# Attention over batches beside an MLP stream on one core: earlier DMA transposes, stores on another queue, single q buffers, a rebalanced start

## The chip, the core and the metric

The kernel runs on one core of a Trainium2 chip. The metric is device microseconds of one execution (us). Most executions of a kernel agree closely; this kernel before the change spreads from 360.9 to 368.7 us. On one core a run counts as slow when it lies over 1.5% above the fastest of the same kernel.

## The reference

Linear attention with cosine and sine weights for 8 batches and 8 heads, sequence 576, head dimension 64, then a low-rank token mixer and a two-layer MLP with a residual. All inputs and outputs are float32.

```python
theta = np.pi / 2.0 * np.arange(S) / S
phi = lambda x: concat([relu(x) * cos(theta), relu(x) * sin(theta)], -1)   # 64 -> 128
q_p, k_p = phi(q), phi(k)                      # (8, 8, 576, 128)
kv  = einsum('bhsf,bhsd->bhfd', k_p, v);  z = sum(k_p, axis=2)
x   = (q_p @ kv) / (q_p . z + 1e-6)            # -> (8, 576, 512)
u   = x + ((x.T @ U) @ V).T                    # rank 32 over the sequence
out = u + relu(u @ w_ch1) @ w_ch2              # 512 -> 2048 -> 512
```

## The kernel before

A main stream of 288 slots runs the MLP on TensorE. Each pair of batches has 72 slots: 32 of `g1_main` (u times w1), 4 of `g1_tail`, 36 of `g2_part` (times w2). After each slot the program may put pieces of a later batch's attention: this is what a plan like `(w + o, thunk)` says, where `w` is the slot at which the batch's `kv` product is placed and `o` the offset. The engines only wait for each other where data or buffers ask for it.

For one batch the chain is: loads of k, v, q; VectorE and ScalarE make `k_p` and `q_p`; `q_p` is transposed by DMA into `q_pT`; TensorE makes `kv`, then `x` from `q_pT` and `kv`, then `A` and `u`; `u_bf` is transposed by DMA into `uT`, which the main stream reads. Both DMA transposes are issued by SyncE.

```python
def alloc_q(b):
    qst[b] = pool.tile([P, H, 4, D], FP32, tag="qst", bufs=2, name="qst")
    qt[b] = pool.tile([P, H, D], FP32, tag="qt", bufs=2, name="qt")
# ... q_p has bufs=1, q_pT bufs=1, kst bufs=2, vst bufs=1
def qtr_dma(b, c0, c1):                      # utr_dma: the same for u_bf -> uT
    # ... c0 < 4:
        nc.sync.dma_start_transpose(
            out=q_pT[b][:, c0:c1, :, :].rearrange("f c h t -> f (c h) t"),
            in_=q_p[b][:, c0:c1, :, :].rearrange("p c h f -> p (c h f)"))
# ... at the end of g2_part: o_sb = u + o_ps, then
            nc.sync.dma_start(out=out[b, 0:512, :]..., in_=o_sb)

def loads(b, eng):                           # kk, vv, qq: a tail and a main load each
    # ... qq(): alloc_q(b); load_tail(qt[b], q, b, eng); load_main(qst[b], q, b, eng=eng)
    return kk, vv, qq

def attention_plan(b):
    plan = [(-6, lambda: v_prep(b))]         # casts of v on GpSimd
    for n, c in enumerate(ORD):
        plan.append((-6 + n, lambda c=c: k_prep(b, c, (V_, V_))))
        plan.append((-6 + n, lambda c=c: q_prep(b, c, (A_, None))))
        plan.append((-5 + n, lambda c=c: q_prep(b, c, (None, A_))))
    plan.append((-3, lambda: qtr_dma(b, 4, 5)))
    plan.append((-1, lambda: qtr_dma(b, 0, 2)))
    plan.append((1, lambda: qtr_dma(b, 2, 4)))
    # ... kv_unit at 0 and 2, x_unit from 6, A_unit at 16, u_unit from 18, utr_dma at 20, 24, 28
    if b + 1 < B:
        for at, t in zip((-5, -2, 2), loads(b + 1, G_)):   # on GpSimd's queue
            plan.append((at, t))
    return plan
# ...
for b, w in ((2, 34), (3, 50), (4, 106), (5, 122), (6, 178), (7, 194)):
    for o, t in attention_plan(b):
        put(w + o, t)
```

Of the kernel before, what the change touches and what calls it, by code (L numbers as in the profile page):

```python
# [10 lines left out]
FP32 = mybir.dt.float32  # L11
# [6 lines left out]
def kernel(  # L18
# [14 lines left out]
    H = 8  # L33
# [34 lines left out]
        vt[b] = pool.tile([P, H, D], FP32, tag="vt", bufs=1, name="vt")  # L68

    def alloc_q(b):  # L70
        qst[b] = pool.tile([P, H, 4, D], FP32, tag="qst", bufs=2, name="qst")
        qt[b] = pool.tile([P, H, D], FP32, tag="qt", bufs=2, name="qt")

    def load_main(dst, src, b, h0=0, h1=H, eng=None):
        (eng or nc.sync).dma_start(
# [88 lines left out]
    V_.memset(q_tl, 0.0)  # L164
    V_.memset(q_tlT, 0.0)
    V_.memset(x_tl, 0.0)
    V_.memset(U_bf, 0.0)
    V_.memset(V_bf, 0.0)

# [67 lines left out]

    def qT_alloc(b):
        if b not in q_pT:
            q_pT[b] = pool.tile([P, 4, H, P], BF16, tag="q_pT", bufs=1, name="q_pT")  # L240

    def qtr_unit(b, c, h0=0, h1=H, eng=None, tag="T", bufs=1):
        qT_alloc(b)
# [39 lines left out]
    def den_unit(b, h0, h1, tag, bufs):  # L283
        n = h1 - h0
        d_ps = ps.tile([P, 5, n], FP32, tag=tag, bufs=bufs, name="d_ps")
        for c in range(5):
            for h in range(h0, h1):
                nc.tensor.matmul(
                    out=d_ps[:, c, h - h0 : h - h0 + 1],
                    lhsT=qT_of(b, c, h),  # L290
                    rhs=kv_sb[b][:, h, D:E],
                    start=True,
                    stop=True,
                )
        rec = pool.tile([P, 5, n], FP32, tag="rec5", bufs=2, name="rec5")
        recip(rec[:, 0:4, :], d_ps[:, 0:4, :])
        recip(rec[tail(b), 4, :], d_ps[tail(b), 4, :])
        return rec

    def xh_unit(b, c, h0, h1, rec, tag, bufs):  # L300
# [183 lines left out]
    def g2_part(pr, cc, part):  # L484

        if part == 0:
            o_ps[pr, cc] = ps.tile([P, DM], FP32, tag="o", bufs=2, name="o_ps")
        o = o_ps[pr, cc]
        if cc == 4:
            lhs, c = hid_tl[pr], 0  # L490
        else:
            b, c = (2 * pr, cc) if cc < 4 else (2 * pr + 1, cc - 5)
            lhs = hid[b]
        for j in range(part * 4, part * 4 + 4):
            nc.tensor.matmul(  # L495
                out=o,
                lhsT=lhs[:, j, c * P : c * P + P],
                rhs=w2_bf[:, j, :],
                start=(j == 0),
                stop=(j == NJ - 1),  # L500
            )
        if part < 3:
            return
        o_sb = pool.tile([P, DM], FP32, tag="o_sb", bufs=3, name="o_sb")
        u = u_tl[pr] if cc == 4 else u_bf[b][:, c, :]
        nc.vector.tensor_tensor(out=o_sb, in0=u, in1=o, op=ALU.add)  # L506
        if cc == 4:
            for i in range(2):
                nc.sync.dma_start(
                    out=out[2 * pr + i, 512:S, :], in_=o_sb[i * TS : i * TS + TS, :]  # L510
                )
        else:
            nc.sync.dma_start(
                out=out[b, 0:512, :].rearrange("(p c) n -> p c n", c=4)[:, c, :], in_=o_sb
            )

# [20 lines left out]

    def attention_plan(b):

        plan = [(-6, lambda: v_prep(b))]  # L540
        for n, c in enumerate(ORD):
            plan.append((-6 + n, lambda c=c: k_prep(b, c, (V_, V_))))
            plan.append((-6 + n, lambda c=c: q_prep(b, c, (A_, None))))
            plan.append((-5 + n, lambda c=c: q_prep(b, c, (None, A_))))
        plan.append((-3, lambda: qtr_dma(b, 4, 5)))
        plan.append((-1, lambda: qtr_dma(b, 0, 2)))
        plan.append((1, lambda: qtr_dma(b, 2, 4)))
        plan.append((0, lambda: kv_unit(b, 0, "T", 1)))
        plan.append((2, lambda: kv_unit(b, 1, "T", 1)))
        for n, c in enumerate(ORD):  # L550
            plan.append((6 + 2 * n, lambda c=c: x_unit(b, c, "X", 1)))
        plan.append((16, lambda: A_unit(b, "T", 1)))
        for n, c in enumerate(ORD):
            plan.append((18 + 2 * n, lambda c=c: u_unit(b, c, "T", 1)))
        if b % 2 == 1:
            plan.append((20, lambda: utr_dma(b, 4, 5)))
        plan.append((24, lambda: utr_dma(b, 0, 2)))
        plan.append((28, lambda: utr_dma(b, 2, 4)))
        if b + 1 < B:
            for at, t in zip((-5, -2, 2), loads(b + 1, G_)):  # L560
                plan.append((at, t))
        return plan


    l1 = loads(1, nc.sync)
    for c in ORD:
        k_prep(0, c, (V_, A_), 0, 4)
    l1[0]()
    for c in ORD:
        q_prep(0, c, (V_, A_), 0, 4)  # L570
    v_prep(0, 0, 4, ORD)
    cast_uv()
    for c in ORD:
        qtr_unit(0, c, 0, 4, A_, "g", 3)
    for c in ORD:
        k_prep(0, c, (V_, A_), 4, 8)
    kv_unit(0, 0, "T", 1)
    for c in ORD:
        q_prep(0, c, (V_, A_), 4, 8)
    l1[2]()  # L580
    rec0 = den_unit(0, 0, 4, "X", 1)
    v_prep(0, 4, 8, ORD, (G_, A_, G_, A_, G_))
    w1_load(0)
    w1_load(1)
    l1[1]()
    for c in ORD[:3]:
        qtr_unit(0, c, 4, 8, A_, "g", 3)
    for c in ORD[:2]:
        xh_unit(0, c, 0, 4, rec0, "o", 2)
    for c in ORD[3:]:  # L590
        qtr_unit(0, c, 4, 8, A_, "g", 3)
    for c in ORD[2:]:
        xh_unit(0, c, 0, 4, rec0, "o", 2)
    kv_unit(0, 1, "T", 1)
    rec1 = den_unit(0, 4, 8, "X", 1)
    a0 = A_unit(0, "X", 1, A_, 0, 256)
    for c in ORD[:4]:
        xh_unit(0, c, 4, 8, rec1, "o", 2)
    for d in range(2):
        uTd_open(0, d, "g", 3)  # L600
        uTd_close(0, d, A_)
    xh_unit(0, 3, 4, 8, rec1, "o", 2)
    uTd_open(0, 2, "g", 3)
    uTd_open(0, 3, "o", 2)
    A_unit(0, "X", 1, V_, 256, 512, a0)
    uTd_close(0, 2, V_)
    uTd_close(0, 3, A_)
    w1_load(2)
    v_prep(1, 0, 8, ORD)
    w1_load(3)  # L610
    for n in range(4):
        w2_load(n)
# [5 lines left out]
        beside.setdefault(j, []).extend(thunks)  # L618

    for n, c in enumerate(ORD):  # L620
        at((0, 0, 1, 1, 2)[n], lambda c=c: k_prep(1, c, (V_, A_)))
        at((3, 4, 5, 6, 7)[n], lambda c=c: q_prep(1, c, (V_, A_)))
        ev = V_ if n % 2 else A_
        tg = ("T", 1) if n % 2 else ("o", 2)
        at((4, 5, 6, 7, 8)[n], lambda c=c, ev=ev, tg=tg: qtr_unit(1, c, eng=ev, tag=tg[0], bufs=tg[1]))
    at(9, lambda: kv_unit(1, 0, "o", 2), lambda: kv_unit(1, 1, "o", 2))
# [2 lines left out]
    xt = (("X", 1), ("o", 2), ("T", 1), ("o", 2), ("X", 1))  # L629
    for n, c in enumerate(ORD):  # L630
        at(10 + n // 2, lambda c=c, t=xt[n]: xh_unit(1, c, 0, 8, rec["r"], *t))
    at(12, lambda: uTd_open(1, 0, "o", 2), lambda: uTd_open(1, 1, "o", 2))
    at(13, lambda: A_unit(1, "T", 1))
    at(13, lambda: uTd_close(1, 0, V_), lambda: uTd_close(1, 1, V_))
    at(14, lambda: uTd_open(1, 2, "o", 2), lambda: uTd_open(1, 3, "X", 1))
    at(14, lambda: uTd_close(1, 2, V_), lambda: uTd_close(1, 3, V_))

    slots, todo = [], {}
    for pr in range(NPAIR):
# [15 lines left out]
        put(18 + n, lambda b=b, c=c: u_unit(b, c, "T", 1))  # L655
    for n, t in enumerate(loads(2, G_)):
        put(16 + n, t)
    for b, w in ((2, 34), (3, 50), (4, 106), (5, 122), (6, 178), (7, 194)):
        for o, t in attention_plan(b):
            put(w + o, t)  # L660
    for i, s in enumerate(slots):
# [33 lines left out]
```

## Time and profile before

| | before |
|---|---|
| median of all its runs at the first comparison (lowest to highest) | 365.44 us (360.90 to 368.74) |
| profiled run: time, span, mean granted TensorE clock (1 is full speed) | 362.37 us, 360.6 us, 0.980 |
| TensorE busy | 316.4 us, 88% of the span |
| `x_ps` on TensorE waiting for `q_pT` | 9.8 us, longest 5.2 |
| `q_pT` transposes, issue to landing (min / median / max) | 4.3 / 5.7 / 15.0 us |
| `uT` transposes, the same | 3.0 / 3.1 / 5.5 us |
| loads by GpSimd, median us to landing: k, v, q | 7.7, 10.4, 12.6 |

How to read it: TensorE is the bound almost throughout, so what counts is where it stands still and where it runs at a lower clock. The main stream makes a natural ruler. I take the time of the first matmul of a slot, and compare slot by slot between kernels.

### The profile page before, as it was taken

The page shows a single profiled execution, that of the slowest core. Times are in us where ns is not written, and L with a number is a line of the kernel's source. Part 1 is how long each engine was busy: PE and PEld are TensorE (multiplying, and loading weights), DVE is VectorE, ACT ScalarE, POOL GpSimd, SP SyncE. Part 2 cuts the span into 40 slices and gives each one's busy share as a digit, 9 for nine tenths or more (in the row PEclk, how much of TensorE's full clock was granted, in tenths as well). Part 3 has the DMA queues.
Part 4 walks back from the last instruction along what each step waited for, and adds up shares of the span by engine and source line. Part 5 has one row for each costly group of instructions (what it writes and reads, how often), then busy time and mean ns, then how long its engine had stood idle before and what let it go on. Part 6 is the DMA issues. An engine that isn't in the chain of part 4 may idle for free.

```text
span 360.6 us, 5601 instructions
## 1 busy us (share of the span) xinstructions
PE 316.4 (88%) x2281; PEld 164.8 (46%) x2281; DVE 148.1 (41%) x328; ACT 146.5 (41%) x256; POOL 66.8 (19%) x109
## 2 busy tenths in 40 slices
PE   0678688999768899999989699999989999999995
PEld 0564354446334444446534344446534444464442
DVE  5645236571753755200585546100585750001121
ACT  3935752569050004769350004669700026661000
POOL 5610920629224300200422300000000000000000
PEclk9999899999969999999999989999999999999999
DMA  8999599599979973634949944004546431000221
GB/s 221 274 264 221 84 198 292 148 299 188 321 197 235 298 167 90 178 99 46 257 106 271 271 131 94 9 0 49 134 93 140 114 97 36 0 0 31 87 84 64
DMA packets 65929, 53.08 MB, mean 147 GB/s; under 512 B 45712, under 2 KB 55984, under 8 KB 65904
## 3 DMA queue, kind: packets, MB, share of 16 engines
q1 hardware_dynamic: 55648, 26.75, 32.1%
q0 software_dynamic: 10256, 25.98, 28.0%
q8 instruction: 18, 0.29, 0.4%
q14 instruction: 7, 0.06, 0.0%
HBM read 36.86 MB, written 9.44 MB: 128 GB/s over the span
## 4 chain that ended last, share of the span: by engine, by line
PE 65%; DMA 14%; ACT 9%; DVE 8%; issue 2%; POOL 0%; SPq 0%; ACTq 0%; DVEq 0%; POOLq 0%
PE g_ps L452 27%; PE o_ps L495 25%; DMA q_pT<-q_p 12%; ACT q_p L195 4%; DMA qt<-in_q_dram 2%; PE a_ps L350 2%; PE va_ps L367 2%; DVE k_p L197 2%; PE kv_ps L229 2%; PE gt_ps L470 2%; PE x_ps L324 2%; ACT hid L459 1%; PE t_ps L246 1%; ACT k_p L195 1%; DVE x_bf L310 1%
## 5 line engine op out<-in xcount | busy, mean ns | idle before, releaser
L459 ACT ACTIVATE hid<-g_ps 128x512 bf16<-128x512 f32 x128 | 76.2, 595 | 140.5 <-PE g_ps L452 140.5
L495 PE MATMUL o_ps<-w_bf,hid 128*128 128x512 bf16 x512 | 122.8, 387 | 0.0
L452 PE MATMUL g_ps<-uT,w_bf 128*128 128x512 bf16 x512 | 117.7, 382 | 0.2
L452 PEld LDWEIGHTS <-w_bf 128*128 128x128 bf16 x512 | 49.9, 98 | 59.9 <-issue 3.5
L495 PEld LDWEIGHTS <-hid 128*128 128x128 bf16 x512 | 48.4, 100 | 53.1 <-issue 3.9
L506 DVE TENSOR_TENSOR o_sb<-u_bf,o_ps 128x512 f32<-128x512 bf16 x32 | 21.9, 684 | 58.1 <-PE o_ps L495 58.1
L105 DVE CAST kv<-kv_ps 128x260 bf16<-128x260 f32 x16 | 6.8, 428 | 64.0 <-PE kv_ps L229 64.0
L368 DVE TENSOR_TENSOR u_bf<-x_bf,va_ps 128x512 bf16<-128x512 bf16 x32 | 22.0, 687 | 22.9 <-PE va_ps L367 22.9
L105 POOL CAST v_ext<-vst 128x512 bf16<-128x512 f32 (+1 forms) x34 | 19.9, 626 | 53.6 <-DMA vst<-in_v_dram 39.3
L195 ACT ACTIVATE q_p<-qst,cosw 128x512 bf16<-128x512 f32 x24 | 17.1, 714 | 20.9 <-DMA q_pT<-q_p 20.9
L195 ACT ACTIVATE q_p<-qst,sinw 128x512 bf16<-128x512 f32 (+1 forms) x36 | 23.4, 666 | 0.0
L324 PE MATMUL x_ps<-kv,q_pT 128*128 128x65 bf16 x192 | 10.8, 200 | 10.6 <-DMA q_pT<-q_p 9.8
L470 PE MATMUL gt_ps<-uT_tl,w_bf 128*128 128x128 bf16 x256 | 16.4, 219 | 2.1 <-ACT hid L459 2.0
L324 PEld LDWEIGHTS <-q_pT 128*128 128x128 bf16 x192 | 9.3, 103 | 18.5 <-DMA q_pT<-q_p 11.3
L229 PE MATMUL kv_ps<-v_ext,k_p 128*128 128x65 bf16 x256 | 12.9, 199 | 4.9 <-DVE A_sb L105 2.4
L470 PEld LDWEIGHTS <-w_bf 128*128 128x128 bf16 x256 | 15.1, 98 | 4.0 <-issue 2.3
L334 DVE TENSOR_TENSOR x_bf<-x_ps,rec 128x512 bf16<-128x512 f32 x24 | 16.6, 691 | 0.8
L197 DVE TENSOR_SCALAR k_p<-kst,cosw 128x512 bf16<-128x512 f32 (+1 forms) x36 | 15.9, 462 | 1.7 <-DMA kst<-in_k_dram 1.5
L229 PEld LDWEIGHTS <-k_p 128*128 128x128 bf16 x256 | 11.8, 102 | 8.3 <-DVE A_sb L105 3.9
L495 PE MATMUL o_ps<-w_bf,hid_tl 128*128 128x512 bf16 x64 | 15.4, 379 | 0.0
L367 PE MATMUL va_ps<-A_sb,V_bf 128*128 128x512 bf16 x40 | 15.1, 378 | 0.0
L246 PE MATMUL t_ps<-ident,q_tl 128*128 128x128 bf16 x16 | 2.0, 276 | 13.7 <-ACT q_tl L195 13.7
(92 smaller groups left out, 251.4 us busy)
## 6 DMA issues: line engine op xcount, KB each, us to landing
out_dram<-o_sb SPq DMA_DIRECT2D x32, 256.0 KB, 2.3
kst<-in_k_dram POOLq DMA_DIRECT2D x6, 1024.0 KB, 7.7
vst<-in_v_dram POOLq DMA_DIRECT2D x6, 1024.0 KB, 10.4
qst<-in_q_dram POOLq DMA_DIRECT2D x6, 1024.0 KB, 12.6
w_bf<-in_moe_w_ch_dram POOLq DMA_DIRECT2D x8, 512.0 KB, 11.0
kst<-in_k_dram SPq DMA_DIRECT2D x2, 512.0 KB, 7.4
qst<-in_q_dram SPq DMA_DIRECT2D x2, 512.0 KB, 8.5
vst<-in_v_dram SPq DMA_DIRECT2D x2, 512.0 KB, 11.0
```

The costliest lines, as they stand in the source:

```text
L105: eng.tensor_copy(out=o, in_=i)
L195: nc.scalar.activation(out=o, in_=i, func=AF.Relu, bias=0.0, scale=w)
L197: eng.tensor_scalar(out=o, in0=i, scalar1=0.0, scalar2=w, op0=ALU.max, op1=ALU.mult)
L229: nc.tensor.matmul(out=acc[:, i, :], lhsT=k_p[b][:, c, h, :] if c < 4 else k_tl[:, h, :], rhs=vx[:, c, h, :], start=(c == 0), stop=(c == 4),)
L324: nc.tensor.matmul(out=acc[:, g, i * E : i * E + E], lhsT=qT_of(b, c, h), rhs=kv_sb[b][:, h, :], start=True, stop=True,)
L367: nc.tensor.matmul(out=va, lhsT=V_bf[:, c, :], rhs=A_sb[b], start=True, stop=True)
L368: nc.vector.tensor_tensor(out=u_bf[b][:, c, :] if c < 4 else u_tl[b // 2][rows, :], in0=x_of(b, c, rows), in1=va[rows, :], op=ALU.add,)
L452: nc.tensor.matmul(out=g_ps.rearrange("p (c t) -> p c t", c=4), lhsT=w1_bf[:, d, j * P : j * P + P], rhs=uT[b][:, :, d, :], start=(d == 0) ...
L459: nc.scalar.activation(out=hid[b][:, j, :], in_=g_ps, func=AF.Relu, bias=0.0, scale=1.0)
L470: nc.tensor.matmul(out=g_ps[:, jj, :], lhsT=w1_bf[:, d, j * P : j * P + P], rhs=uT_tl[pr][:, d, :], start=(d == 0), stop=(d == 3),)
L495: nc.tensor.matmul(out=o, lhsT=lhs[:, j, c * P : c * P + P], rhs=w2_bf[:, j, :], start=(j == 0), stop=(j == NJ - 1),)
L506: nc.vector.tensor_tensor(out=o_sb, in0=u, in1=o, op=ALU.add)
```

## The change

Its intent: get the q transposes issued 16 to 24 slots before their first use instead of 9 to 11; keep SyncE's queue for them by moving the stores to ScalarE's queue; pay for a second `q_pT` buffer by giving up the second buffers of `qst` and `qt`; shorten the start by moving work between engines and keep TensorE's clock up with matmuls on zeros.

```diff
     def alloc_q(b):
-        qst[b] = pool.tile([P, H, 4, D], FP32, tag="qst", bufs=2, name="qst")
-        qt[b] = pool.tile([P, H, D], FP32, tag="qt", bufs=2, name="qt")
+        qst[b] = pool.tile([P, H, 4, D], FP32, tag="qst", bufs=1, name="qst")
+        qt[b] = pool.tile([P, H, D], FP32, tag="qt", bufs=1, name="qt")
@@ qT_alloc
-            q_pT[b] = pool.tile([P, 4, H, P], BF16, tag="q_pT", bufs=1, name="q_pT")
+            q_pT[b] = pool.tile([P, 4, H, P], BF16, tag="q_pT", bufs=2, name="q_pT")
@@ g2_part (both stores)
-            nc.sync.dma_start(
+            nc.scalar.dma_start(
@@ attention_plan
-        plan = [(-6, lambda: v_prep(b))]
+        p0 = {2: -14, 3: -14}.get(b, -20 if b % 2 == 0 else -16)
+        plan = [(p0, lambda: v_prep(b))]
         # ... k_prep and q_prep at p0 + n instead of -6 + n (batch 2: half of q_prep on VectorE)
-        plan.append((-3, lambda: qtr_dma(b, 4, 5)))
-        plan.append((-1, lambda: qtr_dma(b, 0, 2)))
-        plan.append((1, lambda: qtr_dma(b, 2, 4)))
+        plan.append((p0 + 2, lambda: qtr_dma(b, 4, 5)))
+        plan.append((p0 + 4, lambda: qtr_dma(b, 0, 2)))
+        plan.append((p0 + 6, lambda: qtr_dma(b, 2, 4)))
         # ... x from 4 (was 6), A at 14 (16), u at 16 + n (18 + 2n), utr at 18, 20, 22 (20, 24, 28)
-            for at, t in zip((-5, -2, 2), loads(b + 1, G_)):
+            for at, t in zip((-13, -12, -8) if b == 2 else (-4, 0, 4), loads(b + 1, G_)):
@@ placing
-    for b, w in ((2, 34), (3, 50), (4, 106), (5, 122), (6, 178), (7, 194)):
+    for b, w in ((2, 38), (3, 54), (4, 88), (5, 124), (6, 160), (7, 196)):
@@ start (cut: about 60 lines)
+    def keep_warm(n, tag, bufs):             # n matmuls of 512 columns on zeros
+    keep_warm(10, "X", 1)
         # ... 2, 3 and 3 more; v casts and evictions of batch 0 moved between ScalarE, VectorE
         # and GpSimd; k_prep(1) before slot 0; one reciprocal per den_unit instead of two
```

More of the change, by code (lines that the diff above doesn't have):

```diff
@@ L166 @@
     V_.memset(x_tl, 0.0)
+    zero = const.tile([P, 512], BF16)
+    G_.memset(zero, 0.0)
+    def keep_warm(n, tag, bufs):
+        w_ps = ps.tile([P, 512], FP32, tag=tag, bufs=bufs, name="w_ps")
+        for _ in range(n):
+            nc.tensor.matmul(out=w_ps, lhsT=zero[:, 0:P], rhs=zero, start=True, stop=True)
     V_.memset(U_bf, 0.0)
@@ L295, in den_unit @@
         rec = pool.tile([P, 5, n], FP32, tag="rec5", bufs=2, name="rec5")
-        recip(rec[:, 0:4, :], d_ps[:, 0:4, :])
-        recip(rec[tail(b), 4, :], d_ps[tail(b), 4, :])
+        recip(rec, d_ps)
         return rec
@@ L512, in g2_part @@
         else:
-            nc.sync.dma_start(
+            nc.scalar.dma_start(
                 out=out[b, 0:512, :].rearrange("(p c) n -> p c n", c=4)[:, c, :], in_=o_sb
@@ L538, in attention_plan @@
     def attention_plan(b):
-        plan = [(-6, lambda: v_prep(b))]
+        p0 = {2: -14, 3: -14}.get(b, -20 if b % 2 == 0 else -16)
+        plan = [(p0, lambda: v_prep(b))]
         for n, c in enumerate(ORD):
-            plan.append((-6 + n, lambda c=c: k_prep(b, c, (V_, V_))))
-            plan.append((-6 + n, lambda c=c: q_prep(b, c, (A_, None))))
-            plan.append((-5 + n, lambda c=c: q_prep(b, c, (None, A_))))
-        plan.append((-3, lambda: qtr_dma(b, 4, 5)))
-        plan.append((-1, lambda: qtr_dma(b, 0, 2)))
-        plan.append((1, lambda: qtr_dma(b, 2, 4)))
+            plan.append((p0 + n, lambda c=c: k_prep(b, c, (V_, V_))))
+            if b == 2:
+                plan.append((p0 + n, lambda c=c: q_prep(b, c, (V_, A_))))
+            else:
+                plan.append((p0 + n, lambda c=c: q_prep(b, c, (A_, None))))
+                plan.append((p0 + n + 1, lambda c=c: q_prep(b, c, (None, A_))))
+        plan.append((p0 + 2, lambda: qtr_dma(b, 4, 5)))
+        plan.append((p0 + 4, lambda: qtr_dma(b, 0, 2)))
+        plan.append((p0 + 6, lambda: qtr_dma(b, 2, 4)))
         plan.append((0, lambda: kv_unit(b, 0, "T", 1)))
@@ L550, in attention_plan @@
         for n, c in enumerate(ORD):
-            plan.append((6 + 2 * n, lambda c=c: x_unit(b, c, "X", 1)))
-        plan.append((16, lambda: A_unit(b, "T", 1)))
+            plan.append((4 + 2 * n, lambda c=c: x_unit(b, c, "X", 1)))
+        plan.append((14, lambda: A_unit(b, "T", 1)))
         for n, c in enumerate(ORD):
-            plan.append((18 + 2 * n, lambda c=c: u_unit(b, c, "T", 1)))
+            plan.append((16 + n, lambda c=c: u_unit(b, c, "T", 1)))
         if b % 2 == 1:
-            plan.append((20, lambda: utr_dma(b, 4, 5)))
-        plan.append((24, lambda: utr_dma(b, 0, 2)))
-        plan.append((28, lambda: utr_dma(b, 2, 4)))
+            plan.append((18, lambda: utr_dma(b, 4, 5)))
+        plan.append((20, lambda: utr_dma(b, 0, 2)))
+        plan.append((22, lambda: utr_dma(b, 2, 4)))
         if b + 1 < B:
-            for at, t in zip((-5, -2, 2), loads(b + 1, G_)):
+            for at, t in zip((-13, -12, -8) if b == 2 else (-4, 0, 4), loads(b + 1, G_)):
                 plan.append((at, t))
@@ L571 @@
     v_prep(0, 0, 4, ORD)
-    cast_uv()
+    w1_load(0)
     for c in ORD:
@@ L576 @@
         k_prep(0, c, (V_, A_), 4, 8)
+    keep_warm(2, "o", 2)
     kv_unit(0, 0, "T", 1)
@@ L580 @@
     l1[2]()
+    keep_warm(3, "o", 2)
     rec0 = den_unit(0, 0, 4, "X", 1)
-    v_prep(0, 4, 8, ORD, (G_, A_, G_, A_, G_))
-    w1_load(0)
+    v_prep(0, 4, 8, ORD, (G_, G_, V_, G_, V_))
+    cast_uv()
     w1_load(1)
     l1[1]()
-    for c in ORD[:3]:
-        qtr_unit(0, c, 4, 8, A_, "g", 3)
+    keep_warm(3, "o", 2)
     for c in ORD[:2]:
         xh_unit(0, c, 0, 4, rec0, "o", 2)
-    for c in ORD[3:]:
-        qtr_unit(0, c, 4, 8, A_, "g", 3)
+    for n, c in enumerate(ORD):
+        qtr_unit(0, c, 4, 8, (A_, A_, V_, A_, V_)[n], "g", 3)
     for c in ORD[2:]:
@@ L594 @@
     kv_unit(0, 1, "T", 1)
+    k_prep(1, 4, (V_, A_))
+    uTd_open(0, 0, "g", 3)
+    uTd_open(0, 1, "g", 3)
     rec1 = den_unit(0, 4, 8, "X", 1)
-    a0 = A_unit(0, "X", 1, A_, 0, 256)
-    for c in ORD[:4]:
-        xh_unit(0, c, 4, 8, rec1, "o", 2)
-    for d in range(2):
-        uTd_open(0, d, "g", 3)
-        uTd_close(0, d, A_)
+    k_prep(1, 0, (V_, A_))
+    a0 = A_unit(0, "T", 1, A_, 0, 256)
+    xh_unit(0, 4, 4, 8, rec1, "o", 2)
+    xh_unit(0, 0, 4, 8, rec1, "o", 2)
+    uTd_close(0, 0, A_)
+    xh_unit(0, 1, 4, 8, rec1, "o", 2)
+    uTd_close(0, 1, A_)
+    xh_unit(0, 2, 4, 8, rec1, "o", 2)
     xh_unit(0, 3, 4, 8, rec1, "o", 2)
+    for c in (1, 2, 3):
+        k_prep(1, c, (V_ if c == 1 else None, A_))
     uTd_open(0, 2, "g", 3)
     uTd_open(0, 3, "o", 2)
-    A_unit(0, "X", 1, V_, 256, 512, a0)
+    A_unit(0, "T", 1, V_, 256, 512, a0)
     uTd_close(0, 2, V_)
     uTd_close(0, 3, A_)
+    for c in (2, 3):
+        k_prep(1, c, (V_, None))
     w1_load(2)
-    v_prep(1, 0, 8, ORD)
+    v_prep(1, 0, 8, ORD, (G_, G_, V_, G_, V_))
     w1_load(3)
@@ L620 @@
     for n, c in enumerate(ORD):
-        at((0, 0, 1, 1, 2)[n], lambda c=c: k_prep(1, c, (V_, A_)))
-        at((3, 4, 5, 6, 7)[n], lambda c=c: q_prep(1, c, (V_, A_)))
-        ev = V_ if n % 2 else A_
+        at((1, 2, 3, 4, 5)[n], lambda c=c: q_prep(1, c, (V_, A_)))
+        ev = A_ if n in (0, 3) else V_
         tg = ("T", 1) if n % 2 else ("o", 2)
@@ L631 @@
         at(10 + n // 2, lambda c=c, t=xt[n]: xh_unit(1, c, 0, 8, rec["r"], *t))
-    at(12, lambda: uTd_open(1, 0, "o", 2), lambda: uTd_open(1, 1, "o", 2))
-    at(13, lambda: A_unit(1, "T", 1))
-    at(13, lambda: uTd_close(1, 0, V_), lambda: uTd_close(1, 1, V_))
+    at(13, lambda: A_unit(1, "T", 1, A_))
+    at(13, lambda: uTd_open(1, 0, "o", 2), lambda: uTd_open(1, 1, "o", 2))
+    at(14, lambda: uTd_close(1, 0, V_), lambda: uTd_close(1, 1, A_))
     at(14, lambda: uTd_open(1, 2, "o", 2), lambda: uTd_open(1, 3, "X", 1))
-    at(14, lambda: uTd_close(1, 2, V_), lambda: uTd_close(1, 3, V_))
+    at(15, lambda: uTd_close(1, 2, V_), lambda: uTd_close(1, 3, A_))
     slots, todo = [], {}
```

## The prediction

> **What bounds the kernel now.** I read the page first (engine shares, the 40 slices), then the chain that ended last, then the span cut at the program's own seams, and last the queues of SyncE and GpSimd.
>
> ```profile
> PE 316.4 (88%) x2281; PEld 164.8 (46%) x2281; DVE 148.1 (41%) x328; ACT 146.5 (41%) x256; POOL 66.8 (19%) x109
> ...
> PE   0678688999768899999989699999989999999995
> ...
> PEclk9999899999969999999999989999999999999999
> ```
>
> TensorE is the bound almost everywhere, so the question is where it idles or runs slowly. I call a slot one step of the main stream: four 512-column matmuls, 0.864 us (the chain has the last 144 in 31.09 us), or a tail step of 16 narrow ones (64 in 3.57 us, 0.893). There are 288 slots, and all attention work hangs beside them. Cutting the span at slots 0, 15, 36, 72, 108, 144, 180, 216 and at the last matmul, the windows view says (each engine's busy us, then clock, DMA share, GB/s):
>
> ```profile
> 10.60:31.41 20.81, 16.04 (x190) 13.03 (x191) 10.50 (x36) 12.10 (x29) 8.28 (x18) 1.00 1.15 272
> 31.41:62.66 31.25, 24.84 (x247) 13.77 (x245) 14.10 (x28) 18.17 (x29) 10.70 (x15) 0.95 0.95 192
> 62.66:85.98 23.32, 22.62 (x176) 12.35 (x174) 13.22 (x24) 15.50 (x27) 12.39 (x18) 1.00 0.79 215
> 85.98:136.62 50.64, 42.55 (x305) 20.82 (x303) 27.68 (x60) 8.66 (x15) 14.64 (x21) 0.93 0.92 236
> 136.62:170.24 33.62, 32.92 (x217) 17.14 (x215) 7.26 (x15) 24.61 (x42) 3.94 (x5) 1.00 0.47 106
> 170.24:217.52 47.28, 41.64 (x303) 20.38 (x301) 26.85 (x60) 8.51 (x15) 11.54 (x17) 0.96 0.78 201
> 217.52:251.14 33.62, 32.93 (x216) 17.12 (x215) 7.14 (x15) 24.61 (x42) 0.00 (x0) 1.00 0.20 32
> 251.14:293.40 42.26, 39.92 (x303) 19.85 (x301) 26.77 (x60) 8.51 (x15) 0.00 (x0) 1.00 0.49 116
> 293.40:356.37 62.97, 62.93 (x340) 30.31 (x337) 8.25 (x13) 21.49 (x36) 0.00 (x0) 1.00 0.15 47
> ```
>
> The busy figure of PE hides slow stretches, so I compare each length with a floor of start-to-start times read from the warm chain. One batch's attention is kv 1.21, x 5 x 0.26, A 1.09, u 5 x 0.216: 4.7 us. Slots 36-72: 31.1 + 8.1 of attention = 39.2 against 50.6, excess 11.4. Slots 108-144: 39.7 against 47.3, excess 7.6. Slots 180-216, the same work with no loads left: 2.6. The three stretches 15-36, 72-108, 144-180: about 1.1 each. The last 63 us: nothing. So 25 us of excess lie after slot 15, 19 of them in two stretches, and the chain names their cause:
>
> ```profile
> 86.74 0.61 ACT q_p L195
> ...
> 87.38 14.75 DMA q_pT<-q_p
> ...
> 102.17 0.62 PE x_ps L324 x8
> 102.79 3.41 PE o_ps L495 x8
> ```
>
> The q transpose takes 14.75 us to land, since the next batch's 3.5 MB load beside it (DMA share 0.92). TensorE idles 5.2 us, and afterwards eight matmuls take 3.41 us, not 1.73: the granted clock from 102 to 105 us was 0.50. The same pair is at 190.86 (14.99 us). SyncE's queue shows why the other transposes start late: they stand behind stores in order.
>
> ```profile
> 90.95 14.75 SPq L513 DMA_DIRECT2D out_dram<-o_sb  x3
> 105.81 1.35 SPq L264 DMA_TRANSPOSE q_tlT<-q_tl  x1
> 107.34 1.73 SPq L259 DMA_TRANSPOSE q_pT<-q_p  x1
> ```
>
> Before slot 15 there is another regime: loads. GpSimd's timeline:
>
> ```profile
> 36.74 2.28 POOL L105 CAST v_ext<-vst 128x512 bf16<-128x512 f32 x4 [6.63 <-DMA vst<-in_v_dram]
> ...
> 65.98 2.29 POOL L105 CAST v_ext<-vst 128x512 bf16<-128x512 f32 x4 [14.21 <-PE uTt_ps L438]
> ```
>
> Batch 1's v lands at 36.7 and batch 2's at 65.9 (issued 45.1, 20.8 us to landing); the releaser named in the second line is wrong. Batch 2's q, issued 50.9, lands near 67-69.
>
> **What the Trainium skill says.** "TensorE: Matmul & The Clock Gate", section "Part 1: The HAM clock gate", says that TensorE runs at half clock by default and again after about 3.4 us idle, and needs about 3.4 us of activity to leave that state. The trace agrees: at 27.8 us a 512-column matmul takes 0.43 us, at 62 us 0.216, though the page prints clock 1.0 in the first slices, so there I trust durations. "DMA: Bandwidth & Descriptors", section "Issuing engines are not separate DMA queues", says that issue from another engine adds no bandwidth; and its section "Anatomy of one DMA" says that a semaphore wait is made on the issuing sequencer. SyncE's 110.7 us of waiting for o_sb before stores agrees. So the own queue removes the order, not the traffic. "SBUF — State Buffer", section "SBUF: two separate sides", says that VectorE's fast modes and GpSimd exclude each other; k_p steps of 0.47 us became 0.75-0.83 at 97.4-98.9 while GpSimd cast v: it agrees.
>
> **The change part by part.**
> Start to slot 0. Ten zero matmuls at half clock (4.3 us) fill the wait up to the first transpose, so the chain's TensorE pieces from 19.3 to 29.4 (t_ps 1.06, kv 1.11, d 0.69, a 1.25, xh and uT 2.4) halve: about -3. The v casts leave ScalarE (-0.6), two evictions go to VectorE (-1.0), recip is merged (-0.35 twice, on path perhaps half). The k prep of batch 1 comes in on both engines, mostly inside waits (+1 to 1.5). Slot 0 at about 28, not 31.4.
> Slots 0-15. The head start is mostly not kept: VectorE now casts two chunks of v of batch 1 ahead of its q prep, in order, and these land at about 36 whatever the order (the first four slices of 9.0 us moved 221, 274, 264 and 221 GB/s, 8.8 MB, and batches 0 and 1 with U, V and three cast parts of w1 are 8.8 MB; the DMA share from 10.6 us on is 1.15). So TensorE does slots 0-4 by 32.3, idles to about 37.8 and goes cold. From there the preps no longer share ScalarE with k: five transposes and four slots in 8.2 us against 10.7. With the merged recip and A ahead of uT, slot 16 starts near 58, not 63.5: -5.5.
> Slots 16-36. Preps of batch 2 start at 24 (time 67), just as its q lands; VectorE gets u 0.69 + k 0.9 + q 0.45 per 1.15 us slot, and va has one bank: stalls 2, less kv moved out (0.6). About 22.8 long; slot 36 at 80.8.
> Slots 36-72. The transposes of batches 2 and 3 now have 14 to 16 slots (about 15 us) before their use: the 6.5 us of waits and about 4 of cold clock go. Floor 39.8; kv of batch 3 and u of batch 2 share bank T at 54-57 (+2), u of batch 3 meets k prep of batch 4 at 70-73 (+1.5), x behind k prep (+0.5). 43.7 long: slot 72 at 124.5.
> Slots 72-108: batch 4 lies here now, beside an idle VectorE. 27.65 + 3.57 + 4.7 + 0.4 = 36.3, +1: slot 108 at 161.8.
> 108-144: 31.1 + 4.4, +2 where u of batch 5 meets k prep of batch 6 at 140-144: 199.3. 144-180: 36.8: 236.1. 180-216: 36.4: 272.5. 216 to the end 63.2, tail 4.2: span about 340. The profiled run took 1.8 us more than its span: 341.5. Stores on ScalarE move no work: 0.35 us each, in stretches where ScalarE is a fifth busy.
> Against the profiled 362.4 this is -21: 5.5 before slot 16, 7 in 36-72, the rest from 108 on, net of what moves between stretches.
>
> **Rivals.**
> (1) The early loads are the bound: the first 67 us already carry their bytes at a full DMA share. For it, the 36.7 and 65.9 landings; against, only VectorE's v cast and q of batch 2 touch them. If nothing before slot 24 is gained: 347.
> (2) VectorE and its single banks become the bound in slots 36-72: about 33 us of work in 40 (9 o_sb, 7 u and 2 A at 0.69, 10 x at 1.1, 4 kv at 0.43, 18 k steps at 0.45), in bursts. For: u, kv and A share one bank. Against: the stretch of 42.26 us before, with as much VectorE work and few loads, lost only 2.6. It would give 346-349.
> (3) ScalarE's in-order wait for o_sb holds back hid evictions at slots 72, 144, 216. Three g banks cover 2.6 us. At most 1-2 us each time: 345.
> (4) The transposes still land late: the slowest took 15.0 us, about the new lead, but they no longer start with a whole batch's loads. If one is late: +3.
> (5) All stalls hide and the clock holds: 334.
>
> **Range and chances.** The terms that I trust (waits and cold clock after slot 36) are about 18 us; the early 5.5 could be 1 or 8, my added stalls 9 could be 4 or 14. Runs before spread from 360.9 to 366.2. So 341.5, 333 to 350. Faster by over 2% means below 357: 0.96; within 2% 0.03; slower 0.01.
>
> **What would show it.** Right: no q_pT wait before x_ps after 60 us; clock 1.00 from slot 16 on; slot 36 near 81, slot 72 near 124, slots 72-108 longer than 33.6; VectorE waiting for the v load until about 36 and a TensorE gap after slot 4; 512-column matmuls at 0.216 before 20 us. Wrong: stretch 36-72 over 46 (then banks or VectorE), hid waiting on a store, transposes landing after their slot, or slot 0 later than 31.

## The result, and the profile after

The changed kernel takes 403.65 us (median of four runs, 401.07 to 407.26) against 365.44 for the kernel before: the ratio is 1.107, with a 95% interval from 1.090 to 1.124. It is 10.7% slower, where I had expected it 6% faster. Ratios here and below are the mean time of one kernel's fast runs over the mean of the other's from the same rounds, so they are not quite the ratio of the medians quoted.

The profiled run (407.26 us) is slow, for it lies 1.5% above the fastest of its kernel. The other three (401.07, 401.69, 405.62) count as fast. Their clocks, 0.924 to 0.932, lie on both sides of its 0.928, so the profile shows what the fast runs do, give or take the 2 to 6 us between them. The page after:

```profile
PE 317.6 (78%) x2273; PEld 163.8 (40%) x2299; DVE 150.0 (37%) x331; ACT 144.4 (36%) x249; POOL 65.6 (16%) x108
...
PE   3783999894883589005999932989999999999995
...
PEclk9998899999898699756999995999999999999999
```

The busy times are those of before within 2 us or so. What grew is the idle time: TensorE has two slices of nothing and several of 2 to 5 tenths in the middle of the run, and the clock falls to 5 to 7 tenths around them. Cut at slots 36, 72, 108 and 144, as in the prediction (window, length, busy us of TensorE, its weight loads, VectorE, ScalarE and GpSimd, then clock, DMA share and GB/s):

```profile
81.90:146.30 64.40, 43.75 (x319) 21.34 (x324) 28.60 (x65) 10.10 (x16) 12.87 (x19) 0.89 1.00 177
146.30:211.10 64.80, 38.56 (x285) 20.56 (x286) 14.28 (x33) 23.91 (x41) 6.85 (x10) 0.82 0.57 84
211.10:264.40 53.30, 37.83 (x229) 17.96 (x233) 21.70 (x46) 9.91 (x16) 8.20 (x12) 0.87 0.77 144
```

These are slots 36 to 72, 72 to 108 and 108 to 144. They carry the whole miss, as the slot starts show:

| start of slot (us) | 0 | 16 | 36 | 72 | 108 | 144 | 180 | 216 | end of span |
|---|---|---|---|---|---|---|---|---|---|
| before | 31.4 | 63.5 | 86.0 | 136.5 | 170.1 | 217.4 | 251.0 | 293.2 | 360.6 |
| predicted | 28 | 58 | 80.8 | 124.5 | 161.8 | 199.3 | 236.1 | 272.5 | 340 |
| after | 27.2 | 59.6 | 81.9 | 146.3 | 211.1 | 264.4 | 302.3 | 338.1 | 405.4 |

Up to slot 36, and stretch by stretch from slot 144 on, the prediction holds within 2 us. Between them it says 118.5 us and the trace says 182.5. The waits of the changed kernel name the cause (engine and tile, what it waited for: us in total, times, longest):

```profile
POOL qt L81 <- ACT q_tl L203: 120.5, 4, 53.7
...
POOL qst L75 <- ACT q_p L203: 39.8, 4, 18.0
...
PE x_ps L331 <- DMA q_pT<-q_p: 31.7, 3, 14.7
PE g_ps L459 <- DMA uT<-u_bf: 24.8, 1, 24.8
```

TensorE waits 56.5 us for four transposes, all in those stretches. And these do not start late: they take long. The chain that ended last (start, us):

```profile
109.08 26.82 DMA q_pT<-q_p
...
155.81 31.55 DMA uT<-u_bf
```

Two more `q_pT` transposes in the same chain take 22.97 and 30.01 us. In the kernel before the slowest took 15.0. The first two lines of the waits above say what else is new: GpSimd, which issues the loads, now stands waiting for the q preparation before it can reuse the single buffers, first for the tail of q (`qt`), then for its main part (`qst`). In the kernel before each of the two waited once, 15.8 and 6.1 us. After the second release GpSimd issues at once, and k and v of the batch after that follow in order. Its timeline shows the moment (start, us, in brackets the wait before it):

```profile
107.83 0.89 POOL L75 DMA_DIRECT2D qst<-in_q_dram  x1 [18.01 <-ACT q_p L203]
...
112.24 0.89 POOL L75 DMA_DIRECT2D kst<-in_k_dram  x1
```

SyncE's queue has the transposes of batch 3, whose preparation GpSimd waited for:

```profile
105.12 15.82 SPq L267 DMA_TRANSPOSE q_pT<-q_p  x2
```

The last preparation step of `q_p` both fills the tile that is to be transposed and frees the buffer that the next q load waits for. So the release of one starts the other. It also feeds itself: `q_p` has one buffer, so batch 3's preparation on ScalarE stood 13.9 us until batch 2's late transpose had landed (102.53), and the loads released by its end then met batch 3's transposes.

Packets show how the two disturb each other. In a stretch of the kernel before where both are in flight, 92 to 100 us, the queues have (packets, MB, share of the 16 DMA engines' time; q0 is GpSimd's, q1 is SyncE's and carries the transposes):

```profile
q0 software_dynamic: 641, 2.36, 94.1%
q1 hardware_dynamic: 632, 0.16, 11.4%
```

In the changed kernel, 156 to 180 us:

```profile
q0 software_dynamic: 796, 2.97, 62.8%
q1 hardware_dynamic: 2311, 0.58, 47.6%
```

Share times 16 engines times the window's length over packets is the time of one: 0.941 x 16 x 8 / 641 = 188 ns for a load packet and 23 ns for a transpose packet in the first, 303 and 79 ns in the second. The rate over the window falls from 316 to 149 GB/s. The loads suffer too: k takes 19.1 us to land (median) where it took 7.7, v 21.7 against 10.4.

### The profile page after: what moved, and what is told of

The parts are those of the page before. It is cut to its first block, busy times and chain, and to the rows that moved or that the text cites. A ratio compares the mean times of both kernels' runs of the same rounds, so it can differ in the third digit from the quotient of the medians.

```text
span 405.4 us, 5603 instructions
## 1 busy us (share of the span) xinstructions
PE 317.6 (78%) x2273; PEld 163.8 (40%) x2299; DVE 150.0 (37%) x331; ACT 144.4 (36%) x249; POOL 65.6 (16%) x108
## 4 chain that ended last, share of the span: by engine, by line
PE 52%; DMA 34%; DVE 6%; ACT 3%; issue 2%; POOL 2%; SPq 1%; ACTq 0%; POOLq 0%; DVEq 0%
PE g_ps L459 22%; DMA q_pT<-q_p 20%; PE o_ps L502 19%; DMA uT<-u_bf 8%; DMA vst<-in_v_dram 4%; PE gt_ps L477 3%; ACT q_p L203 2%; DMA vt<-in_v_dram 2%; PE va_ps L374 2%; DVE k_p L205 2%; DVE u_bf L375 2%; PE a_ps L357 2%; PE x_ps L331 2%; PE kv_ps L237 1%; PE t_ps L254 1%
## 5 line engine op out<-in xcount | busy, mean ns | idle before, releaser
L459 PE MATMUL g_ps<-uT,w_bf 128*128 128x512 bf16 x512 | 121.8, 385 | 25.6 <-DMA uT<-u_bf 24.8
L502 PE MATMUL o_ps<-w_bf,hid 128*128 128x512 bf16 x495 | 119.7, 389 | 0.8
L459 PEld LDWEIGHTS <-w_bf 128*128 128x128 bf16 x512 | 48.9, 99 | 88.0 <-issue 37.2
L502 PEld LDWEIGHTS <-hid 128*128 128x128 bf16 x512 | 49.4, 100 | 58.0 <-issue 6.4
L331 PE MATMUL x_ps<-kv,q_pT 128*128 128x65 bf16 x192 | 10.8, 201 | 32.7 <-DMA q_pT<-q_p 31.7
L203 ACT ACTIVATE q_tl<-qt,cosw 64x512 bf16<-64x512 f32 x5 | 3.6, 718 | 79.9 <-DVE o_sb L513 79.8
L81 POOL DMA_DIRECT2D qt<-in_q_dram x7 | 5.6, 804 | 125.3 <-ACT q_tl L203 120.5
L288 DVE TENSOR_SCALAR rec<-x_ps 128x8 f32<-128x8 f32 (+1 forms) x30 | 4.9, 165 | 54.5 <-PE x_ps L331 54.5
L105 POOL CAST v_ext<-vst 128x512 bf16<-128x512 f32 (+1 forms) x32 | 17.8, 597 | 17.4 <-PE va_ps L374 13.4
L203 ACT ACTIVATE q_p<-qst,cosw 128x512 bf16<-128x512 f32 x20 | 14.2, 709 | 13.9 <-DMA q_pT<-q_p 13.9
L477 PEld LDWEIGHTS <-w_bf 128*128 128x128 bf16 x256 | 15.1, 98 | 1.7
## 6 DMA issues: line engine op xcount, KB each, us to landing
kst<-in_k_dram POOLq DMA_DIRECT2D x6, 1024.0 KB, 19.1
vst<-in_v_dram POOLq DMA_DIRECT2D x6, 1024.0 KB, 21.7
```

Source lines behind the costliest of these rows:

```text
L105: eng.tensor_copy(out=o, in_=i)
L203: nc.scalar.activation(out=o, in_=i, func=AF.Relu, bias=0.0, scale=w)
L331: nc.tensor.matmul(out=acc[:, g, i * E : i * E + E], lhsT=qT_of(b, c, h), rhs=kv_sb[b][:, h, :], start=True, stop=True,)
L459: nc.tensor.matmul(out=g_ps.rearrange("p (c t) -> p c t", c=4), lhsT=w1_bf[:, d, j * P : j * P + P], rhs=uT[b][:, :, d, :], start=(d == 0) ...
L477: nc.tensor.matmul(out=g_ps[:, jj, :], lhsT=w1_bf[:, d, j * P : j * P + P], rhs=uT_tl[pr][:, d, :], start=(d == 0), stop=(d == 3),)
L502: nc.tensor.matmul(out=o, lhsT=lhs[:, j, c * P : c * P + P], rhs=w2_bf[:, j, :], start=(j == 0), stop=(j == NJ - 1),)
```

## The experiments

Theory A: the single q buffers make the loads on GpSimd's queue fall together with the transposes on SyncE's, and transposes and loads in flight together on two queues slow each other. Theory B: the stores on ScalarE's queue do it. Theory C: the new plan does, by what it puts beside what. All kernels below gave correct results. Each was timed in four runs beside runs of the kernel before, whose median was 361.9 to 363.2 us in these rounds.

### 1. The buffers undone

```diff
 changed kernel
-  qst, qt: bufs=1      q_pT: bufs=2
+  qst, qt: bufs=2      q_pT: bufs=1
```

> The changed kernel with its three buffer counts undone (q load buffers 2 again, q_pT 1 again). Theory A (the single q load buffer ties the next batch's loads to the very moment at which the transposes go out, and in that mix both crawl): the loads run earlier, the q and u transposes land in under 15 us (were 23 to 32), time falls to about 365 or less. Theory B (the third DMA queue with the stores is what slows the mix) and theory C (the new places in the plan are): little changes, 395 to 405 us, and waits of over 10 us for q_pT stay.

Measured: 374.91 us (371.21 to 376.92), ratio 1.029 [1.017, 1.040]. That gains 29 us, but the kernel is still slower than before (the interval lies above 1): TensorE waits 9.2 us for `q_pT` and 11.2 for `uT`, and a transpose still takes up to 20.6 us. So the buffers are a large part and not all. My figure for theory A, 365 at most, was missed.

### 2. The stores back on SyncE

```diff
 changed kernel
-  nc.scalar.dma_start(out=out..., in_=o_sb...)
+  nc.sync.dma_start(out=out..., in_=o_sb...)
```

> The changed kernel with the stores back on SyncE's queue. Theory B (stores on a queue of their own disturb transposes and loads): falls to 365 or less. Theory A or C: 400 or more, as transposes now also stand behind stores again; the 31 us landing of a u transpose beside no store stays.

Measured: 401.83 us (392.73 to 412.79), with such a spread that no ratio is given: three of the four count as slow, and the one fast run is the 392.73. That is far from the 365 of theory B, so as the main cause it falls; a gain of some us is not excluded by this run alone (experiments 8 and 14 find none). The waits change their names: TensorE's 18.3 and 16.2 us for VectorE's `x_bf` and `x_tl` lead back to VectorE, which stood 18.9 and 17.4 us for stores of `o_sb` to land, and these are now in SyncE's queue with the transposes.

### 3. The plan undone

```diff
 changed kernel
-  the new attention_plan; w = 38, 54, 88, 124, 160, 196
+  the attention_plan of before; w = 34, 50, 106, 122, 178, 194
```

> The changed kernel with the plan of batches 2 to 7 undone (offsets and places), new buffers, store queue and early part kept. Theory C (the plan makes it slow): 350 to 362, below the kernel before by the early gain. Theory A (single q buffer): stays at 380 or more, since q of batch b+1 still waits for the q preps of batch b.

Measured: 409.58 us (403.55 to 412.27), ratio 1.117 [1.103, 1.131]. TensorE waits 44.4 us for `q_pT`. Theory C falls: with the old plan the loss is as large.

### 4. The early part alone

```diff
 kernel before
+  zero tile, keep_warm; batch 0's chain rebalanced; k_prep(1) before slot 0; one recip
```

> The kernel before with only the early part of the change (zero matmuls, batch 0 chain, merged recip, batch 1 beside the first slots). My prediction said 5.5 us off at slot 16; all theories expect that to hold here: about 355 to 359 us against 361 to 366, slot 16 near 60 us as in the changed kernel. If it is no faster, the early gain is given back later even without the other parts.

Measured: 366.06 us (364.79 to 367.34), ratio 1.007 [0.998, 1.015]. I had expected 355 to 359. Slot 16 does start 3.5 us earlier (60.0 against 63.5), but the gain is given back in the next stretch, between slots 36 and 72. Most of it goes at the `x_ps` step that the prediction shows at 102.17 us, where TensorE had waited 5.16 us. In this kernel (start, us, in brackets the wait before it):

```profile
101.57 0.62 PE L331 MATMUL x_ps<-kv,q_pT 128*128 128x65 bf16 x8 [7.30 <-DMA q_pT<-q_p]
```

The transpose beside the loads lands only 0.6 us sooner, so TensorE waits longer for it. The next transpose of the stretch holds `x_ps` until 126.93 us (126.65 before), and from 120 us to slot 72 the clock is 0.83 against 1.00, so that slot 72 starts 3.2 us later than before. In all TensorE waits 15.1 us for `q_pT`, against 9.8. The early part's time is lost in these waits.

### 5. Only the single q buffers, on the kernel before

```diff
 kernel before
-  qst, qt: bufs=2
+  qst, qt: bufs=1
```

> The kernel before with one single edit: the q load buffers (main and tail) from 2 to 1. Theory A (this buffer alone makes the change slow, as it holds GpSimd's in-order queue until the q preps of the batch before are read, and so sends the loads out together with the transposes): 385 us or more, transposes landing after 20 us or more. If the second q_pT buffer is the cause, or the two only together: 358 to 370.

Measured: 385.44 us (383.09 to 391.53), ratio 1.061 [1.047, 1.075]. Two lines, with nothing else of the change, cost 22 us. `q_pT` takes up to 31.7 us to land, and TensorE waits for it 25.9 us where it waited 9.8. This is theory A's number.

### 6. One q_pT buffer again

```diff
 changed kernel
-  q_pT: bufs=2
+  q_pT: bufs=1
```

> The changed kernel with q_pT back to one buffer and the single q load buffer kept. Theory A: 395 to 410, as the changed kernel. If the second q_pT buffer is the cause: 375, as with both undone.

Measured: 406.64 us (400.88 to 412.15), ratio 1.111 [1.096, 1.126]. The second `q_pT` buffer does nothing here. Of the three buffer lines those of `qst` and `qt` count.

### 7. The loads issued by SyncE

```diff
 changed kernel
-  loads(b + 1, G_)
+  loads(b + 1, nc.sync)
```

> The changed kernel with the loads of batches 3 to 7 issued on SyncE's queue, in program order between the transposes, instead of GpSimd's. Loads and transposes then share one queue[...]. If the slow landing comes from loads and transposes in turns on the same engines (theory A's second half): transposes land in 4 to 10 us, and the time falls below 360, towards the 341 predicted. If the DMA engines simply have too much to do, or SyncE's in-order queue now holds the transposes: 390 or more.

Measured: **344.80 us** (343.66 to 345.14), ratio 0.949 [0.942, 0.955]. It beats both kernels, by one word changed. SyncE's queue is in order, so the loads now go out behind the transposes:

```profile
94.91 6.45 SPq L267 DMA_TRANSPOSE q_pT<-q_p  x2
...
102.17 0.58 SPq L75 DMA_DIRECT2D kst<-in_k_dram  x1
```

`q_pT` lands after 4.3 to 8.2 us, `uT` after 3.0 to 9.5, k after 8.5 (median), and TensorE has no wait for a DMA after 60 us. The three stretches of the miss (slots 36 to 72, 72 to 108, 108 to 144), with the same columns as above:

```profile
83.40:127.30 43.90, 40.41 (x318) 20.45 (x322) 28.33 (x65) 10.21 (x16) 4.62 (x9) 1.00 0.97 210
127.30:165.70 38.40, 37.00 (x285) 19.95 (x286) 14.29 (x33) 23.91 (x41) 2.90 (x5) 1.00 0.60 144
165.70:202.20 36.50, 35.76 (x229) 17.42 (x233) 21.46 (x46) 9.93 (x16) 2.84 (x5) 1.00 0.83 209
```

I had predicted 43.7, 37.3 and 37.5 for the change itself. The loss of the changed kernel closes here: its stretches are 182.5 us long, these 118.8, a difference of 63.7. The four waits for transposes are 56.5 of it, and TensorE's busy time is 120.1 against 113.2, 6.9 us, at a clock of 0.82 to 0.89 against 1.00. That makes 63.4.

### 8. Buffers and stores undone together

```diff
 changed kernel
-  qst, qt: bufs=1   q_pT: bufs=2   stores on nc.scalar
+  qst, qt: bufs=2   q_pT: bufs=1   stores on nc.sync
```

> The changed kernel with the three buffer counts and the store queue undone: early part and new plan alone. The run with the buffers undone took 375. If the store queue is worth its place there: 380 or more here; if the stores on their own queue cost: 366 or less.

Measured: 373.52 us (372.43 to 374.24), ratio 1.028 [1.021, 1.035], the same as with the buffers alone undone (374.91). What still lies above experiment 7 is not the store queue, as either gives the same time. Only the waits differ: here TensorE waits 9.4 us for `uT`, and 13.3 us for `x_bf` and `x_tl`, which again lead back to stores that land late (VectorE stands 15.0 us for them).

### 9. The loads stay on GpSimd, but are held back

A small copy on GpSimd that reads this batch's `kv` must run before the next batch's loads, so they can't be issued before that product. Only the time of issue changes, not the queue.

```diff
 changed kernel
+  if b > 2:
+      plan.append((0, lambda: G_.tensor_copy(out=guard, in_=kv_sb[b][:, 0, 0:1])))
-  zip((-13, -12, -8) if b == 2 else (-4, 0, 4), loads(b + 1, G_))
+  zip((-13, -12, -8) if b == 2 else (0, 0, 4), loads(b + 1, G_))
```

> The changed kernel, all loads still on GpSimd's queue, with one tiny GpSimd copy that reads kv of batch b before the loads of batch b+1 (b from 3 on), so that these go out at slot w of batch b, some 14 slots after its q transposes, and not together with them. If the overlap in time of loads and transposes on two queues is the cause (theory A): 345 to 360, transposes of batches 4 to 7 landing in under 10 us; batch 3 is not helped. If loads from GpSimd are slow in themselves whatever the moment: 390 or more.

Measured: 355.92 us (355.50 to 357.17), ratio 0.981 [0.976, 0.985], so 48 us less than the changed kernel with no change of queue. From slot 72 to the end it takes 216.1 us, experiment 7 takes 216.0: on GpSimd's queue too, loads that keep clear of the transposes cost nothing. The 11 us that remain all lie before slot 72. There, loads issued from 106 to 111 us still meet the `uT` transposes issued at 108.5 and 112.3, which take 25.9 and 26.1 us to land, and TensorE waits:

```profile
PE g_ps L460 <- DMA uT<-u_bf: 12.2, 1, 12.2
```

### 10. One queue, but loads among the transposes

```diff
 experiment 7
-  zip((-13, -12, -8) if b == 2 else (-4, 0, 4), loads(b + 1, nc.sync))
+  zip((p0 + 3, p0 + 3, p0 + 5), loads(b + 1, nc.sync))
```

> The loads of batches 3 to 7 on SyncE's queue as in the 345 us run, but placed right among the q transposes of the batch before (k and v ahead of the first big one, q between the two). If two queues taking turns on the DMA engines are needed for the slow landing: 343 to 352, no wait of over 3 us for q_pT or uT[...]. If nearness in time alone does it, whatever the queue: 365 or more.

Measured: 369.65 us (364.25 to 371.37), ratio 1.009 [1.000, 1.017]. I had leant to 343 to 352 and was wrong: nearness in time costs 25 us on a single queue as well (22 if only the two fast runs, 364.25 and 368.35, are taken). The landings, up to 13.7 us for `q_pT` and 9.4 for `uT`, are much shorter than the 30.0 and 31.5 on two queues, and TensorE waits 17.9 us for them against 56.5. Here loads also stand ahead of transposes in the same order, so part of this is plain queueing. So the two-queue mix is worse, though the loads do not stand at the same places in the two kernels; and keeping them apart is what experiment 9 shows to be worth 48 of the 59 us.

### 11. Experiment 7 with the start of before

```diff
 experiment 7
-  early part of the change
+  early part of the kernel before
```

> The 345 us run with the early part of the change undone (no zero matmuls, the old batch 0 chain and first 16 slots). The prediction's 5.5 us at slot 16 should now be worth its full size at the end, since no late transpose gives it back: 348 to 352. If the early part is worth nothing here too: 343 to 346.

Measured: 346.85 us (346.35 to 347.30), ratio 0.955 [0.952, 0.959]. The early part is worth 2 us (344.80 against 346.85), not the 5.5 that I had given it and not the 3 to 7 that I expected of this run. At slot 16 the two kernels are 2.5 us apart (61.1 and 63.6).

### 12. The kernel before, with only its queues changed

```diff
 kernel before
-  loads(b + 1, G_)        stores on nc.sync
+  loads(b + 1, nc.sync)   stores on nc.scalar
```

> The kernel before with its old plan and buffers, its loads of batches 3 to 7 moved to SyncE and its stores to ScalarE. If the mix on two queues was also what bound the kernel before (its transposes landed after 15 us with TensorE idle for 5 us): 345 to 355. If its transposes are late because they are issued late: 358 to 365.

Measured: 350.90 us (350.61 to 353.21), ratio 0.968 [0.963, 0.972]. TensorE's wait for `q_pT` shrinks from 9.8 to 2.3 us, so late transposes held the kernel before as well. The run moves loads and stores together: it does not separate the mix of two queues from the place of the transposes behind the stores, and experiments 8 and 14, where the store queue made no difference, have the new plan. The new plan, the buffers and the start together are worth 6 us more.

### 13. Loads among the transposes, issued by ScalarE

```diff
 experiment 10
-  loads(b + 1, nc.sync)
+  loads(b + 1, A_)
```

> As g2_sp_overlap (loads placed among the q transposes of the batch before, 370 us on SyncE's own queue), but the loads are issued by ScalarE, so on another queue than the transposes, though not on GpSimd's. If any second queue makes the mix slow: 385 or more, transposes landing after 15 us or more. If it takes GpSimd's queue: 365 to 375, or less as the transposes no longer stand behind the loads.

Measured: 393.26 us (386.91 to 395.99), without a ratio. The time is in the range that I had put down for "any second queue", but the waits do not bear it out. TensorE's longest in total is this:

```profile
PE g_ps L459 <- ACT hid L466: 14.4, 7, 5.0
```

Next come 9.3 and 7.1 us for VectorE's `x_bf` and `x_tl`. The first is for ScalarE's own work, which shares its instruction stream with the loads; for a transpose TensorE waits 1.8 us in all, though landings go up to 18.3. The other two lead back to the stores, which ScalarE issues too: VectorE stood 8.9 and 8.3 us just before for a store of `o_sb` to land. The run mixes several effects and decides nothing.

### 14. Experiment 7 with the stores on SyncE

```diff
 experiment 7
-  stores on nc.scalar
+  stores on nc.sync
```

> The 345 us run with the stores back on SyncE too, so that loads, transposes and stores share one queue in order. If the store queue matters once loads are in order: 350 or more, as transposes and loads wait behind stores for o_sb; else 343 to 347.

Measured: 345.00 us (344.38 to 345.76), ratio 0.951 [0.943, 0.959]. The queue of the stores makes no difference in this kernel.

### 15. Experiment 7 with the buffers of before

```diff
 experiment 7
-  qst, qt: bufs=1   q_pT: bufs=2
+  qst, qt: bufs=2   q_pT: bufs=1
```

> The 345 us run with the three buffer counts undone (two q load buffers, one q_pT). If the single q buffer hurts only by timing the loads on GpSimd's queue, it is harmless here and undoing it gains nothing: 343 to 350 (over 345 where the single q_pT makes the transposes of one batch wait for the x of the batch before). If it costs in itself: below 342.

Measured: 344.39 us (343.65 to 346.34), ratio 0.950 [0.943, 0.957]. A single q buffer, which cost 22 us in experiment 5 and 29 in experiment 1, costs nothing once the loads are on SyncE. With experiment 9, where it stays single and only the moment of the loads changes, this says that it does harm through the moment at which it lets the loads go.

All slot starts of the runs that the argument rests on:

| start of slot (us) | 16 | 36 | 72 | 108 | 144 | 216 | end of span |
|---|---|---|---|---|---|---|---|
| 1 buffers undone | 60.4 | 83.0 | 135.4 | 187.3 | 230.4 | 304.1 | 371.4 |
| 4 early part alone | 60.0 | 82.8 | 139.6 | 173.5 | 222.3 | 298.2 | 365.6 |
| 5 before, single q buffers | 64.3 | 86.8 | 153.8 | 187.6 | 238.1 | 314.0 | 381.4 |
| 7 loads on SyncE | 61.1 | 83.4 | 127.3 | 165.7 | 202.2 | 275.9 | 343.3 |
| 9 loads held back | 59.6 | 82.1 | 138.4 | 176.9 | 213.4 | 287.1 | 354.5 |
| 10 one queue, near | 61.4 | 83.6 | 129.9 | 175.5 | 219.3 | 299.2 | 366.6 |
| 12 before, queues changed | 63.5 | 85.9 | 128.2 | 162.0 | 208.1 | 284.0 | 351.4 |

## Why the prediction was wrong, point by point

**The step that failed.** In slots 36 to 72 the prediction says: "The transposes of batches 2 and 3 now have 14 to 16 slots (about 15 us) before their use: the 6.5 us of waits and about 4 of cold clock go." The transposes did get their lead, and needed 23 to 32 us. The same step, unsaid, carries the sums for 72 to 108 and 108 to 144. Its error is 20.7 + 27.5 + 15.8 = 64.0 us out of a total miss of 65.4 in the span.

**What stood behind it.** Rival 4 saw the danger ("the transposes still land late") and set it aside, for "they no longer start with a whole batch's loads". I read that from the slots at which the diff places the loads. GpSimd does not run by slots: it runs ahead until something stops it (in the kernel before, the loads of batch 4, placed at slots 45 to 52, went out from 84.8 to 89.0 us, and slot 36 starts at 86.0). What stops it in the changed kernel is the single q buffer, and this lets it go exactly when the transposes go out. I gave the two buffer lines no cost. Experiments 5, 1 and 15 show what they do: 22 us on the kernel before, 29 in the changed kernel, nothing with the loads on SyncE.

**The size of rival 4.** I allowed 3 us for a transpose that comes late, measured by the 15.0 us of the slowest one in the trace before. That was the landing in a stretch where the two queues shared the engines at 316 GB/s. In the changed kernel the same mix ran at 149 GB/s.

**The own queue for the transposes.** The prediction says that a queue of their own "removes the order, not the traffic". The first half made no difference that shows (experiments 8 and 14; experiment 2 spreads too much to tell). The second half was the whole matter, and I did not follow it to a number.

**What held.** Slot 0 at 27.2 (28 predicted), slot 36 at 81.9 (80.8). VectorE waits for batch 1's v until 36.09 us, 7.4 us long, and TensorE stands still after slot 4, as foretold. The stretch from slot 180 to 216 is 35.8 us long (36.4), from 216 to the last matmul 63.1 (63.2). Ten zero matmuls took 3.66 us (4.3), and eight transposes on TensorE behind them 0.80, where 1.06 was to halve. With the loads kept off the transposes, the tuned kernel of experiment 7 ends at 343.3 where I had put the change at 340. The rest of the working thus comes out about right under that one condition. But part of this nearness is luck: on the kernel before, the queues alone bring 350.9 us (experiment 12), so of the 18 us that experiment 7 gains, the change's own parts are worth 6.

**Small slips.** By the diff the transposes of batches 2 and 3 go out 16 to 18 slots before their first use, not 14 to 16, and the matmul quoted at 27.8 us is at 27.4 (the piece at 27.8 is four narrow ones). Neither moves a sum.

**The early gain.** Slot 16 gained 3.9 us, not 5.5. As part of the working kernel it is worth 2 (experiment 11); on the kernel before it was worth nothing, since the next waits on transposes absorbed it (experiment 4).

**The other rivals.** The early loads (1) took part of the gain at slot 16, but not all of it. VectorE's banks (2) did not come: in experiment 7, with the same plan, TensorE has no wait over 1 us for VectorE's `u_bf` and 3.7 us of them in all. Nor did ScalarE's queue (3): with the stores back on SyncE the time is the same (experiment 14).

**What stays open.** Shown is that loads near transposes make both slow, that of the pairings tried GpSimd's queue with SyncE's had the longest landings, and that keeping them apart in time cures it on either queue. Not shown is why such a mix ran at 316 GB/s in one stretch and at 149 in another. Whether any second queue behaves like GpSimd's is open too, as experiment 13 is blurred by ScalarE's own waits. Nor is it explained why the old plan with single buffers and the new start (experiment 3) loses 24 us more than the old kernel with single buffers (experiment 5). I would guess that it depends on which load meets which transpose, but no run separates this.

## What to carry to other kernels

A buffer that becomes single is also a release: ask at which event the waiting engine will go on, what it will then start, and what that will meet. An engine that does little runs ahead of its place in the program, so place its transfers by what it waits for, not by the line where they stand. If a kernel uses DMA transposes on its critical path, issue the bulk loads from the same in-order queue behind them, or hold the loads back with a real dependency, and check the landing times in the profile before working on anything else.

## What the Trainium skill lacked or had wrong

- "DMA: Bandwidth & Descriptors", section "Issuing engines are not separate DMA queues", says that issuing from several engines "will only save the time on the sequencer". It leaves out that the issuing engine also decides when and in what order the transfers go out: the same loads issued by SyncE instead of GpSimd took the changed kernel from 403.65 to 344.80 us, and the kernel before, with its stores moved as well, from 362.9 to 350.9. Most of the first gain is this moment and order, since holding the loads back on GpSimd gave 355.9.
- The same page, section "Rules for kernel authors", says that "A transpose next to ordinary DMAs needs nothing". All results were correct, so this holds for correctness. For time it does not: transposes that took 3 to 6 us (medians before) took up to 31.5 beside loads on another queue, the loads' median went from 7.7 to 19.1 us, a load packet from 188 to 303 ns and a transpose packet from 23 to 79 ns. No page gives a cost for this mix.
- The same page, section "SWDGE vs HWDGE vs iDMA", assigns plain loads and transposes to SyncE or ScalarE and leaves GpSimd the casting ones. The kernels before and after break this with float32 loads on GpSimd. Following it with SyncE gained the 59 us of experiment 7, but 48 of them came in experiment 9 without it, and loads near the transposes from ScalarE took 393.26 us (experiment 13). The page gives no number for the choice and says nothing of where in the queue to put the loads.
- No page draws from the separate instruction streams of the engines that a buffer count decides when an engine with little to do starts its loads: here two lines of buffer counts cost 22 us alone (385.44 us).
